# Eight more transpose sets in 64 by 64 tiles, and the steps reordered around them, in a retention and WaveMLP kernel

## The chip, the cores and the metric

The kernel runs on one core of a Trainium2 chip. The metric is the device time of one execution in microseconds (us). The engines are named as the profile names them: PE is TensorE (matmul, and transposes as matmuls against an identity), PEld its weight loads, DVE is VectorE, ACT is ScalarE, POOL is GpSimd, SP is SyncE, which here issues DMAs only. ACT and POOL issue some DMAs as well.

## The reference

A recurrent retention layer (4 batches, 8 heads, 768 positions, 64 numbers a head) feeds a mixing layer of width 512:

```
state = gamma[h] * state + outer(k[t], v[t])        # for each batch and head
y[t]  = (q[t] @ state) / sqrt(64)
x     = y, heads side by side                       # 4 x 768 x 512
theta = x @ w_theta
zr, zi = x * cos(theta), x * sin(theta)
u     = x + w_tok_r @ zr + w_tok_i @ zi             # mixes the 768 positions
out   = u + relu(u @ w_ch)
```

Inputs and output are float32.

## The kernel before

**Tiling.** The recurrence is computed in blocks. A *unit* n covers one batch, 256 positions and four heads: three blocks of positions (i = 0, 1, 2) and two halves of the heads (h) for each of four batches make 24 units. The mixing layer works on *chunks* C of 128 positions, 6 to a batch and 24 in all; output tiles t are numbered in the same way. The units 2m and 2m+1 make the chunks 2m and 2m+1.

**Steps of a unit.** `Lk`, `Lq`, `Lv` load k, q and v (tiles kqf and vf, 256 KB a load). `ck` casts k to bf16 (tile kqb), `cq` casts q, `cqs` casts q and multiplies it by its decay, `cv` does so for v (tile vb). `Tk` and `Tq` transpose k and q on PE with four 128 by 128 transposes each; `E` empties the result from PSUM into kqT. Some units go another way: `Dk` transposes by a DMA, and `Tk6`, `Tq6`, `E6` do what `Tk`, `Tq`, `E` do in 64 by 64 tiles, below. `A` multiplies k by q (sixteen 64 by 64 products, tile at_ps), `m` masks it (DVE, tile at). `ST` makes the block's state (r_ps), `S0` and `S1` add it to the running state (s2), `SB` casts that state into a block-diagonal tile (sbd), `I` multiplies it by q, and `Y` adds at times vb. `XA` (times a decay, qx) or `XB` (a plain copy, if q was scaled by `cqs`) takes the result from PSUM into xT.

**Steps of a chunk.** `Tx` and `Ex`, `Tx6` and `Ex6`, or a transposing DMA `Dx` bring xT into x_sb. `Hh` multiplies xT by w_theta (four products, th_ps); `CN` takes sine and cosine (ACT, tile cs, two calls of 128x512); `z` multiplies them by x. `Tw`, `Tw6` and `Ew`, `Ew6` transpose the token weights, one set for each 128 columns of the two matrices. `M.t.s` is one sixth of output tile t (two products, y_ps), `u` adds x, `Tu`, `Tu6` or a transposing DMA `Du` transposes u, `O` multiplies by w_ch, `f` adds the relu, `SO` stores. The last tile is done in halves (`Mh`, `uh`, `Tuh`, `Oh`, `fh`). `Z` is an empty product on zeros that feeds nothing.

**64 by 64 tiles.** `tiles64` (line 331) does each 128 by 128 transpose as four transposes of 64 by 64, each on a quarter of the array. The results go to two PSUM tiles, one for each half of the source's partitions, and each is emptied by its own copy. PSUM tiles of transposes come from a pool with two buffers (tag "tr"): a full set takes one of them, a set in 64 by 64 tiles takes both. `A`, `ST` and `Y` use 64 by 64 tiles anyway.

**Order.** Nothing is scheduled by rule. The table ORDER lists some 940 steps by hand; the last part of a name tells the engine (v DVE, a ACT, p POOL) or the queue of a load or store (s SP, a ACT). Each engine and each queue runs its own steps in the order of the table and waits in place. So a load on SP that stands behind a transposing DMA also waits for what that DMA waits for. PSUM banks for `Hh`, `M` and `O` come from a pool of two (tag "acc").

**Constants.** const3 computes the small decays (qsc, vsc) and const8 and const9 the large one (qx) with exponentials on ACT; const7 is one small sine, so that the sine's table is loaded there. An exponential and a sine need different tables; the load is an instruction of its own.

## Time and profile before

| | |
|---|---|
| median of 3 runs | 164.59 us (164.54 to 165.16) |
| span of the profiled execution | 163.3 us |
| granted clock of PE | 1.000 |
| bytes moved by DMA | 35.19 MB |

The time of the profiled execution itself is not given; the runs lie 1.2 to 1.9 us above its span, the median 1.3. The page lists busy time by engine and the costliest groups of instructions. Matmuls are pipelined: the duration of one holds some time in which the next runs already, so the cost of a step on PE is read from the start of one group to the start of the next. The other engines overlap neighbours by a little less than 0.1 us.

### The profile page before, as it was taken

To read this page: it belongs to the slowest core of one execution; us is meant where nothing else is said; L and a number is where in the kernel's file an instruction comes from. 1 tells how busy PE (TensorE), PEld (TensorE's weight loads), DVE (VectorE), ACT (ScalarE), POOL (GpSimd) and SP (SyncE) were. 2 spreads that over 40 slices of the span, in tenths; PEclk is the share of its full clock that TensorE was granted. 3 is DMA by queue.
4 is the path that set the end of the run, shared out by engine and by line. 5 is a ranking of instruction groups with operands and counts; after the bars stand their busy time and mean duration, and the time that the engine had idled before them with its cause. 6 is when DMAs were issued, how large, how long until landed. Compare 5 with 4: busy or idle time off the path is not lost.

```text
span 163.3 us, 5070 instructions
## 1 busy us (share of the span) xinstructions
PE 154.7 (95%) x2100; PEld 85.5 (52%) x2100; DVE 114.5 (70%) x217; ACT 78.8 (48%) x147; POOL 74.3 (45%) x106
## 2 busy tenths in 40 slices
PE   5996989999999998999999999999999999999992
PEld 1454646656666654644544655455545554444561
DVE  3388687987994786794999787698867760345362
ACT  4966698983658264673423645822341616000020
POOL 7657289176514770520057689910469204600000
PEclk9999999999999999999999999999999999999999
DMA  4999999999999999999999999999896527514446
GB/s 116 297 290 252 258 294 240 277 220 285 226 162 275 296 205 220 251 207 245 335 236 172 242 195 305 222 192 276 185 251 129 101 64 225 161 68 128 128 156 230
DMA packets 70118, 35.19 MB, mean 215 GB/s; under 512 B 27472, under 2 KB 67152, under 8 KB 70096
## 3 DMA queue, kind: packets, MB, share of 16 engines
q1 hardware_dynamic: 57088, 24.00, 68.6%
q10 hardware_dynamic: 10320, 7.47, 16.6%
q0 software_dynamic: 2688, 3.41, 12.1%
q8 instruction: 16, 0.26, 0.7%
q14 instruction: 6, 0.05, 0.1%
HBM read 25.69 MB, written 6.29 MB: 196 GB/s over the span
## 4 chain that ended last, share of the span: by engine, by line
PE 79%; DMA 7%; DVE 6%; POOL 4%; issue 1%; ACT 1%; DVEq 0%; POOLq 0%
PE y_ps L559 33%; PE o_ps L595 10%; PE th_ps L511 10%; PE zz L279 5%; PE r_ps L458 4%; PE at_ps L380 4%; DMA x_sb<-xT 4%; DMA kqT<-kqb 3%; PE kq_ps L318 3%; PE w_ps L533 2%; DVE at L389 2%; POOL z L525 2%; PE r_ps L446 2%; PE y_ps L620 2%; PE r_ps L408 1%
## 5 line engine op out<-in xcount | busy, mean ns | idle before, releaser
L559 PE MATMUL y_ps<-z,wtr 128*128 128x512 bf16 x138 | 52.4, 380 | 0.0
L559 PE MATMUL y_ps<-z,wti 128*128 128x512 bf16 x138 | 52.3, 379 | 0.0
L525 POOL TENSOR_TENSOR z<-cs,x_sb 128x1024 bf16<-128x1024 bf16 x12 | 25.5, 2135 | 17.7 <-ACT cs L518 10.8
L389 DVE TENSOR_TENSOR at<-at_ps,mask 128x1024 bf16<-128x1024 f32 x24 | 29.2, 1215 | 0.5 <-PE at_ps L380 0.5
L310 POOL TENSOR_TENSOR vb<-vf,vsc 128x512 bf16<-128x512 f32 x15 | 15.6, 1045 | 21.7 <-ACT sbd L136 11.7
L601 DVE SCALAR_TENSOR_TENSOR ot<-o_ps,u 128x512 f32<-128x512 f32 x22 | 15.1, 688 | 13.6 <-PE o_ps L595 13.5
L511 PE MATMUL th_ps<-wth,xT 128*128 128x512 bf16 x96 | 24.5, 380 | 0.0
L566 DVE TENSOR_TENSOR u<-y_ps,x_sb 128x512 bf16<-128x512 f32 x23 | 15.8, 688 | 10.9 <-PE y_ps L559 10.5
L595 PE MATMUL o_ps<-wch,uT 128*128 128x512 bf16 x88 | 22.6, 380 | 0.0
L518 ACT ACTIVATE cs<-th_ps,halfpi 128x512 bf16<-128x512 f32 x24 | 16.3, 682 | 11.8 <-PE th_ps L511 7.0
L518 ACT ACTIVATE cs<-th_ps,zerob 128x512 bf16<-128x512 f32 x24 | 16.4, 684 | 10.6 <-PE th_ps L511 5.1
L559 PEld LDWEIGHTS <-wtr 128*128 128x128 bf16 x138 | 13.5, 98 | 13.4
L559 PEld LDWEIGHTS <-wti 128*128 128x128 bf16 x138 | 13.5, 98 | 12.7 <-issue 0.4
L138 POOL CAST sbd<-s 64x256 bf16<-64x256 f32 (+1 forms) x20 | 8.4, 418 | 24.3 <-DVE s L426 22.1
L136 ACT COPY kqT<-kq_ps 128x1024 bf16<-128x1024 bf16 (+1 forms) x10 | 9.7, 969 | 9.8 <-PE kq_ps L318 9.5
L511 PEld LDWEIGHTS <-xT 128*128 128x128 bf16 x96 | 8.7, 98 | 8.5
L279 PE MATMUL zz<-zero 128*128 128x512 bf16 x30 | 10.8, 495 | 1.9 <-DVE zero L191 1.9
L595 PEld LDWEIGHTS <-uT 128*128 128x128 bf16 x88 | 8.1, 98 | 8.4 <-issue 0.2
L136 ACT CAST kqb<-kqf 128x512 bf16<-128x512 f32 x16 | 9.6, 620 | 5.5 <-DMA kqf<-in_k_dram 5.4
L458 PE MATMUL r_ps<-at,vb 64*64 64x128 bf16 x384 | 10.0, 221 | 1.6 <-DVE at L389 1.6
L380 PE MATMUL at_ps<-kqT 64*64 64x128 bf16 x384 | 10.0, 220 | 1.1 <-DVE kqT L138 0.6
L476 DVE TENSOR_TENSOR xT<-r_ps,qx 128x256 bf16<-128x256 f32 x22 | 8.7, 417 | 1.8 <-PE r_ps L458 0.8
(88 smaller groups left out, 209.4 us busy)
## 6 DMA issues: line engine op xcount, KB each, us to landing
vf<-in_v_dram SPq DMA_DIRECT2D x20, 256.0 KB, 5.7
kqf<-in_k_dram SPq DMA_DIRECT2D x19, 256.0 KB, 5.4
kqf<-in_q_dram SPq DMA_DIRECT2D x17, 256.0 KB, 5.7
out_dram<-ot ACTq DMA_DIRECT2D x12, 256.0 KB, 2.5
out_dram<-ot SPq DMA_DIRECT2D x11, 256.0 KB, 2.4
kqf<-in_q_dram ACTq DMA_DIRECT2D x7, 256.0 KB, 5.4
kqf<-in_k_dram ACTq DMA_DIRECT2D x5, 256.0 KB, 6.7
vf<-in_v_dram ACTq DMA_DIRECT2D x4, 256.0 KB, 5.7
```

Source lines behind the costliest of these rows:

```text
L136: nc.scalar.copy(dst, src)
L279: nc.tensor.matmul(t[:m, :cols], K["zero"][:, :m], K["zero"][:, :cols], start=True, stop=True)
L310: engines[e].tensor_mul(in_blocks(vb), by_token(raw["vf", n]), _bcast_last(K["vsc"][:, i, :, h * HU:(h + 1) * HU], D))
L380: nc.tensor.matmul(at_ps[cols, g, j, a, :], kq_at(n, 0, a, j, c)[rows], kq_at(n, 1, slice(0, 2), j, c)[rows], start=(j == 0 and a == 0), s ...
L389: nc.vector.tensor_mul(at.rearrange("p g j a t -> p (g j) (a t)"), st["at_ps", n].rearrange("p g j a t -> p (g j) (a t)"), _bcast_mid(K["m ...
L458: nc.tensor.matmul(st["R", n + 1][c][g * D:(g + 1) * D, j * P:(j + 1) * P], st["vb", n][rows, lo:lo + D], st["at", n][rows, g, j, a, :], s ...
L511: nc.tensor.matmul(th_ps, st["xT", C][:, j, :], K["wth"][:, j, :], start=(j == 0), stop=(j == 3))
L518: nc.scalar.activation(st["cs", C][:, w, :], st["th_ps", C], AF.Sin, bias=K["zerob" if w else "halfpi"], scale=1.0)
L525: engines[e].tensor_mul(st["z", b][:, c], st["cs", C], _bcast_mid(x_of(C), 2))
L559: nc.tensor.matmul(st["y", t], K["wT"][r][:, s0, t0 * P:(t0 + 1) * P], st["z", b][:, s0, r, :], start=(done == 0 and r == 0), stop=(done = ...
L566: nc.vector.tensor_add(st["u", t], st["y", t], st["x", b][:, t0, :])
L595: nc.tensor.matmul(o_ps, st["uT", t][:, j, :], K["wch"][:, j, :], start=(j == 0), stop=(j == nD - 1))
```

## The change

The functions that do the work are the same. What changes is the table: 936 steps become 944. Two new functions, `SP` and `I6`, stand in the code and are not in the table. Line numbers shift by one, and by 17 behind the new functions.

- **Sets in 64 by 64 tiles.** k and q of units 0 to 3 (`Tk`, `Tq`, `E` become `Tk6`, `Tq6`, two `E6` each), `Tw.1.2` and `Tw.1.4`. Chunks 1, 8 and 15 use `Tx6`, and chunk 12 goes back to `Tx`: two more. For u the four sets in 64 by 64 tiles are now 0, 3, 5 and 8, before 4, 5, 8 and 11.
- **Fewer changes of tiling.** In the order of the table PE changes between full tiles and 64 by 64 tiles 60 times from the first set to the last, before 68 times.
- **Engines.** z of chunks 0, 13, 15, 22 and 23 goes from POOL to DVE; many casts and copies change engine. Units 0, 7, 9, 12 and 21 take `cq` and `XA` where they had `cqs` and `XB`, and units 5, 6 and 19 the other way round.
- **Order.** Almost every step stands elsewhere. The loads on SP keep their order up to the loads of unit 12.

```diff
-const2 Lv.0.s const1 const6.v Z.29 Z.2 const5 Z.38 Lk.0.a const3 Z.35 Z.8 Lq.0.s Lv.1.s Z.28 constA
-const4 Lq.1.a const9 Lk.1.s Z.39 const8 ck.0.p Tk.0 ck.1.a cqs.0.v cv.0.v Tq.0 E.0.v Lq.4.a ST.0 Lk.4.a
...
+Lv.0.s Lk.0.a const2 const1 Lq.0.s Z.3 Z.11 const5 Lv.1.s ck.0.v Z.23 Lq.1.a cq.0.v const3 Lk.1.s Z.38
+Lq.4.a constA const4 const7 cqs.1.p cv.0.v Z.15 Tk6.0 const8 ST.0 Tq6.0 const6.v Z.18 E6.0.0.a Z.8
...
+    def SP(n, e):
+        _, i, h = unit(n)
+        c0 = 0 if i else 1
+        st["sp", n] = work.tile([P, 2, 2, D], BF, name="sp", bufs=3)
+        copy(e, st["sp", n][:, c0:], st["s2", n][:, c0:])
+
+    def I6(n):
+        r = R_of(n + 1)
+        for pair in (((0, 1), (1, 0)), ((0, 0), (1, 1))):
+            for j in range(2):
+                for g, c in pair:
+                    rows = slice(g * D, (g + 1) * D)
+                    nc.tensor.matmul(r[c][rows, j * P:(j + 1) * P], st["sp", n][rows, c, j, :],
+                                     kq_at(n, 1, slice(0, 2), j, c)[rows],
+                                     start=(j == 0), stop=False, skip_group_check=True)
```

Two places as the built programs have them. First the start of ACT's queue, before. (qsc and vsc are const3, qx is const8 and const9, one is const7; a row named DMA is a load that ACT issues.)

```order
L239 ACT_TABLE_LOAD
L239 ACTIVATE qsc<-arg,lscale 128x48
L239 ACTIVATE vsc<-arg,zerob 128x48
L156 DMA kqf<-in_q_dram 128x4x128
L232 ACTIVATE qx<-pos,lscale,lgp 128x512 x4
L232 ACTIVATE qx<-pos,lscale,lgp 128x256 x4
L136 CAST kqb<-kqf 128x512
L156 DMA kqf<-in_q_dram 128x4x128
L156 DMA kqf<-in_k_dram 128x4x128
L136 COPY kqT<-kq_ps 128x1024
```

And now, the same queue:

```order
L240 ACT_TABLE_LOAD
L240 ACTIVATE qsc<-arg,lscale 128x48
L240 ACTIVATE vsc<-arg,zerob 128x48
L157 DMA kqf<-in_q_dram 128x4x128
L252 ACT_TABLE_LOAD
L252 ACTIVATE one<-zerob,halfpi 128x1
L233 ACT_TABLE_LOAD
L233 ACTIVATE qx<-pos,lscale,lgp 128x256 x4
L137 COPY kqT<-kq_ps 128x512 x2
L157 DMA kqf<-in_k_dram 128x4x128
L233 ACTIVATE qx<-pos,lscale,lgp 128x512 x4
```

The sine has moved from behind the exponentials to between them, so that two more table loads stand in the queue (the fourth follows later, ahead of the first `CN`); the load of q of unit 4 has moved ahead of the exponentials, and that of k of unit 4 stays behind the first eviction.

Second, the queue of SP around the load of q of unit 10, which is the same before and now but for the numbers. Now (u_1280 is u.1, kqf_1399 is q of unit 10, kqf_1440 q of unit 14):

```order
L157 DMA kqf_1152<-in_k_dram 128x4x128
L607 DMA_TRANSPOSE uT_1342<-u_1280 128x4x128
L157 DMA kqf_1399<-in_q_dram 128x4x128
L607 DMA_TRANSPOSE uT_1429<-u_1292 128x4x128
L157 DMA kqf_1440<-in_q_dram 128x4x128
```

What moved is its user. On PE before, `Tq.10` (kqb_1158) stands behind two steps of M.4 (y_ps_1320):

```order
L559 MATMUL y_ps_1320<-z_738,wtr_101 128x512
L559 LDWEIGHTS wti_102
L559 MATMUL y_ps_1320<-z_738,wti_102 128x512
L318 LDWEIGHTS kqb_1158
L318 MATMUL kq_ps_1315<-ident_159,kqb_1158 128x128
```

And now (kqb_1328) behind `Tk.10` and the first step of M.3 (y_ps_1451):

```order
L319 LDWEIGHTS kqb_1328
L319 MATMUL kq_ps_1446<-ident_158,kqb_1328 128x128
L576 LDWEIGHTS wtr_103
L576 MATMUL y_ps_1451<-z_839,wtr_103 128x512
L576 LDWEIGHTS wti_104
L576 MATMUL y_ps_1451<-z_839,wti_104 128x512
L319 LDWEIGHTS kqb_1328
L319 MATMUL kq_ps_1446<-ident_158,kqb_1328 128x128
```

`Tq.10` has moved ahead of all other steps of M.3 and of the whole of M.4. At the same time the last step of M.1, for which u.1 waits, has moved back behind `A.8`; before, it stood ahead of `Tk.8`.

## The prediction

> **What bounds the kernel now.** I read the page's busy shares first, then the windows by stretch, then TensorE's (PE's) own timeline with its waits, and last the queues in front of the two places where PE waits.

> ```profile
> PE 154.7 (95%) x2100; PEld 85.5 (52%) x2100; DVE 114.5 (70%) x217; ACT 78.8 (48%) x147; POOL 74.3 (45%) x106
> ```
> ```profile
> 8.00:12.00 4.00, 3.79 (x90) 2.33 (x88) 3.24 (x7) 2.39 (x5) 2.15 (x4) 1.00 1.22 290
> 12.00:16.00 4.00, 2.50 (x66) 1.58 (x66) 3.14 (x7) 3.00 (x6) 3.18 (x5) 1.00 1.20 258
> 22.20:32.00 9.80, 9.56 (x172) 6.07 (x172) 8.43 (x17) 9.12 (x16) 6.26 (x8) 1.00 1.17 268
> 32.00:64.00 32.00, 32.00 (x429) 18.87 (x426) 25.66 (x51) 19.11 (x33) 16.98 (x16) 1.00 1.16 237
> ```
> The columns are the stretch, its length, then busy time and count of PE, PE's weight loads, DVE, ACT, POOL, then the granted clock, the DMA share and GB/s. From 32 on PE never rests and the clock is 1.00: there each microsecond of PE work is a microsecond of time. Ahead of 22 PE rests or is fed with empty products; between 22 and 32 ACT is busy 9.12 of 9.80 and sets the pace as much as PE does.

> ```profile
> L279 PE MATMUL zz<-zero 128*128 128x512 bf16 x30 | 10.8, 495 | 1.9 <-DVE zero L191 1.9
> ```
> ```profile
> 14.27 0.42 PE L458 MATMUL r_ps<-at,vb 64*64 64x128 bf16 x16 [1.11 <-DVE at L389]
> 21.68 0.42 PE L458 MATMUL r_ps<-at,vb 64*64 64x128 bf16 x16 [0.47 <-DVE at L389]
> 31.41 1.03 PE L511 MATMUL th_ps<-wth,xT 128*128 128x512 bf16 x4
> 64.90 0.42 PE L380 MATMUL at_ps<-kqT 64*64 64x128 bf16 x16 [0.49 <-DMA kqT<-kqb]
> ```
> The bracket is PE's idle time ahead of the row and what ended it. The third row is Hh.4, my milestone. The fourth is the longest wait after it.

> **The change part by part.** *Transposes and tiling.* What a set costs, and what a change of tiling costs:

> ```profile
> 38.53 0.61 PE L318 MATMUL kq_ps<-ident,kqb 128*128 128x128 bf16 x8
> 38.98 0.38 PE L559 MATMUL y_ps<-z,wtr 128*128 128x512 bf16 x1
> ...
> 68.12 0.42 PE L337 MATMUL kq_ps<-ident,kqb 64*64 64x64 bf16 x32
> 68.37 0.31 PE L408 MATMUL r_ps<-vb,kqb 64*64 64x64 bf16 x16
> ```
> ```profile
> 65.32 0.22 PE r_ps L458 x16
> 77.52 3.02 PE y_ps L559 x14
> 80.55 0.35 PE r_ps L458 x16
> 81.55 0.97 PE o_ps L595 x4
> 152.35 0.86 PE o_ps L595 x4
> ```
> From start to start, k and q of one unit cost 0.45 in full tiles and 0.25 in 64 by 64 tiles. In the second fence (the chain of waits: start, length) the same sixteen products take 0.22 behind 64 by 64 work and 0.35 behind full tiles, and the same four 0.97 against 0.86: 0.13 to enter, 0.11 to leave. Four k, q sets give 4 x 0.20 = 0.8; two x sets half as much each, 0.2; two weight sets of 24 small transposes (24 of 32 of the 0.25, 0.19) instead of 6 full ones (6 of 8 of the 0.45, 0.33) 0.14 each, 0.3: together 1.3. By the order table PE's tiling changes 60 times now, 68 before; 8 x 0.12 = 0.9. Sum: 2.2 of PE work less. But when I add PE's steps in program order by these durations, Hh.4 has 126.5 of work behind it before and 126.3 now. So 2.0 of the 2.2 lie ahead of Hh.4, where other things pace the kernel; they count only as far as those chains get shorter.

> *Evictions.* A set is now emptied in two halves, and both banks of the pool are taken.

> ```profile
> L136 ACT COPY kqT<-kq_ps 128x512 bf16<-128x512 bf16 x1 | 0.6, 585 | 0.3 <-PE kq_ps L337 0.3
> L136 ACT COPY kqT<-kq_ps 128x1024 bf16<-128x1024 bf16 x9 | 9.1, 1011 | 9.5 <-PE kq_ps L318 9.5
> L136 ACT CAST kqb<-kqf 128x512 bf16<-128x512 f32 x16 | 9.6, 620 | 5.5 <-DMA kqf<-in_k_dram 5.4
> L136 ACT CAST sbd<-s 64x256 bf16<-64x256 f32 x12 | 4.8, 403 | 1.9 <-DVE s L426 1.7
> L136 ACT CAST xT<-r_ps 128x256 bf16<-128x256 f32 x17 | 5.9, 374 | 7.1 <-DVE s L426 4.7 <-PE r_ps L408 1.2 <-PE r_ps L458 1.1
> ```
> Two halves cost ACT 1.17 instead of 1.01, 0.16 a set. Where the PE has other work (after Hh.4) this is covered by it; without that cover it is 0.16 a set.

> *ACT's tables.* const7 (the sine that loads its table early) now stands ahead of the exponentials of const8 and const9, so the order on ACT has four table loads, not two.

> ```profile
> 1.67 1.28 ACT L239 ACT_TABLE_LOAD   x1 [1.67 <-DVE arg L216]
> 13.48 1.28 ACT L251 ACT_TABLE_LOAD   x1
> 23.23 0.69 ACT L518 ACTIVATE cs<-th_ps,zerob 128x512 bf16<-128x512 f32 x1
> 23.81 0.68 ACT L518 ACTIVATE cs<-th_ps,halfpi 128x512 bf16<-128x512 f32 x1
> ```
> The second and third load (2.57) stand while the first inputs are still landing; the fourth stands straight ahead of the first sine, behind unit 3's xT. It is on the path, since ACT is the full engine there: 1.28. [...]

> *From the fifth unit's q to Hh.4.* In the vector queue cqs.5 now stands ahead of S0.4 and m.4, so all wait for q of unit 5.

> ```profile
> 3.21 0.32 ACT L239 ACTIVATE vsc<-arg,zerob 128x48 f32<-128x48 f32 x1
> 8.70 0.44 ACTq L156 DMA_DIRECT2D kqf<-in_q_dram  x1
> 9.18 0.53 ACTq L156 DMA_DIRECT2D kqf<-in_k_dram  x1
> 15.85 0.37 SPq L156 DMA_DIRECT2D kqf<-in_k_dram  x1
> 16.26 0.51 SPq L156 DMA_DIRECT2D kqf<-in_q_dram  x1
> ```
> ```profile
> DMA to landing us min/median/max: 5.7/5.7/5.7
> ```
> ```profile
> 6.07 0.69 DVE L304 TENSOR_TENSOR kqb<-kqf,qsc 128x512 bf16<-128x512 f32 x1 [3.11 <-DMA kqf<-in_q_dram]
> 22.26 0.29 DVE L426 TENSOR_TENSOR s<-r_ps,s 128x128 f32<-128x128 f32 x1 [0.63 <-PE r_ps L408]
> ```
> The first fence is ACT's and SP's, the second the landing of q of unit 5: 16.26 and 5.7, so 21.96. The third has DVE's price of a scaled cast and of a state add. SP issues k of unit 5 (15.85) and q behind it only when k of unit 4 (9.18) has landed. Now q of unit 4 is issued right behind vsc, at 3.5 instead of 8.70, so one load less stands in k of unit 4's way: 0.26 MB at 290 GB/s (first window) is 0.9. Bounds: 0, if only bytes count, and 1.6, if all SP loads move up as far as k of unit 4 can. I take 1.2, nearer to the upper end, since the windows show GB/s falling from 290 to 258 while SP waits: there is room. So q lands at 20.8, cqs.5 and S0.4 end at 21.7 (0.69 and 0.29). Then ACT in its new order, each about 0.1 less than its row because neighbours overlap (23.23 to 23.81 is 0.58 for a 0.69): sbd 0.32, two xT 0.56, table 1.28, sines of C 1 1.17, kqb 0.52, sines of C 0 1.17, sbd 0.32, kqT 0.92, sines of C 2 and C 3 2.44: 8.7. Hh.4 needs the bank that C 3's sines empty: 30.4 against 31.41. With 0.2 less work behind it: **1.2 gained**, 0.0 if q lands as before, 1.6 at best.

> *q of unit 10.* Here the reordering puts something on the path. On SP this load stands behind the transposing DMA Du.1, which waits for u.1, the vector add behind the last product of M.1.

> ```profile
> 42.71 0.68 DVE L566 TENSOR_TENSOR u<-y_ps,x_sb 128x512 bf16<-128x512 f32 x1
> 43.42 1.28 SPq L590 DMA_TRANSPOSE uT<-u  x1
> 44.80 0.53 SPq L156 DMA_DIRECT2D kqf<-in_q_dram  x1
> 52.32 1.04 POOL L304 TENSOR_TENSOR kqb<-kqf,qsc 128x512 bf16<-128x512 f32 x1
> 55.21 0.39 PE L318 MATMUL kq_ps<-ident,kqb 128*128 128x128 bf16 x4
> ```
> ```profile
> DMA to landing us min/median/max: 6.2/6.2/6.2
> ```
> ```profile
> DMA to landing us min/median/max: 4.2/4.2/4.2
> ```
> The rows are u.1, Du.1, the load, cqs.10 and Tq.10; the landing of this load, and that of the next one (issued 48.21). The chain is fixed: 0.2 for the product's end, u.1 0.7, Du.1's issue 1.4, landing, cqs.10 1.05, with 0.1 for hand-overs 3.5 plus the landing, 7.7 to 9.7. In the order table PE had 13.6 of work between the last product of M.1 and Tq.10: hidden, as 55.21 against the landing at 51.0 shows. Now M.1 ends later and Tq.10 comes earlier: M.2 four times (1.73; a step M is two products of 0.216, the 3.02 for fourteen above), Hh.6, Hh.7, O.0 (2.59), Tx.6, Tk.9, Tq.9, Tk.10 (0.89), Tw.0.3, I.8 (0.56), one 64 by 64 group (1.0), M.3.0 (0.43): 7.2. PE, in order, waits 0.5 to 2.5 with everything behind it. I take 5.2 for the landing, midway: **1.5 lost**. Nothing else ahead of PE has so short a lead.

> *What comes back.* A wait on PE lets the DMA chains behind it catch up:

> ```profile
> 59.39 5.47 DMA kqT<-kqb
> ```
> This transfer made the 0.49 at 64.90. cq.11 now runs on POOL and issues it some 0.5 later within its chain, but PE is later by more: I count the 0.5 back. z of five chunks moves from POOL to DVE, which at 25.66 of 32 (fourth window) has room; I put it at 0, with bounds of -0.5 (the size of the one wait that a late buffer made) and +0.5.

> Sum against the profiled execution: 163.3 - 1.2 + 1.5 - 0.5 = 163.1. The runs' median of 164.59 lies 1.3 above its span: **164.4**.

> **The rivals.** *The load is hidden after all.* If it lands in 4.2, as the next one did, the wait is 0.5; with 1.2 to 1.6 from the front and the 0.5 back: 163.0 to 163.4, say 163.2. For it: the row of 4.2. Against: the load beside it took 6.2 while a large weight load was still running.

> *The loads do not come earlier* (slower). q of unit 5 lands at 21.96 again, Hh.4 starts at 31.5 and gains 0.1; u.1 is then as late as PE, and with a landing of 6.2 Tq.10 waits 2.5; 0.5 comes back: 164.6 - 0.1 + 2.5 - 0.5 = 166.5, or 165.8 with a middling landing; I say 166.0. It decides from a q of unit 5 later than about 21.6. For it: DMA share over 1.1 in every window to 64. Against: the falling GB/s. [...]

> *The change does not save what it says*: the two-bank sets make PE wait for both halves of each eviction, 0.16 by the rows above for each of the eight sets, 1.3 on top of the 164.4: 165.7. Against: after Hh.4 PE has other work ahead of each next set.

> **How the numbers follow.** Within 0.5% (163.8 to 165.4, about what a measurement of this kernel can tell from no change) lies the forecast, 0.36; the hidden load, faster, 0.36; the loads that stay, 0.20, and the double eviction, 0.08, slower, 0.28. The range of eight in ten runs from 163.0 to 166.0; the forecast's own is 163.8 to 165.2.

> **What would show it.** Right: PE's longest wait after 32 is ahead of Tq.10 at about 52, ended by POOL's kqb; no wait at A.11; four table loads, the last just ahead of the first cs; Hh.4 near 30.4. Wrong: Tq.10 without a bracket, Hh.4 after 31, or long waits of PE ended by kqT, x_sb or z between 60 and 150.

## The result, and the profile after

The changed kernel takes 169.35 us (median of 4 runs, 168.99 to 169.92), the kernel before 164.56 (4 runs): a ratio of 1.0289, 95% interval 1.0256 to 1.0322. It is slower by 4.8 us, where 164.4 was forecast. Times and ratios below leave out runs that lie over 1.5% above the fastest of their kernel (two of four in a_full, one of four in b_many, two of six in b_t6_01 and in b_tail, one of six in b_t6_01z and in b_t6_23z); a ratio can still differ a little from the quotient of two medians.

The page after gives the busy time and the clock of PE in 40 slices of 4.2 us:

```profile
PE 153.1 (92%) x2225; PEld 86.2 (52%) x2256; DVE 121.2 (72%) x231; ACT 74.2 (44%) x141; POOL 66.4 (40%) x108
...
PEclk9999579999999999999999999999999999999998
```

The span is 4.0 longer (167.3 against 163.3). What grew is rest, and work at a lower clock. How much less PE works cannot be read from this page: 31 of its 2256 products are missing in this trace (x2225, against x2256 weight loads), while the trace before has all of its 2100. The windows, with the columns of those before:

```profile
12.00:16.00 4.00, 2.21 (x92) 1.42 (x83) 3.58 (x9) 3.56 (x8) 1.91 (x2) 1.00 1.21 293
16.00:22.20 6.20, 4.94 (x118) 3.52 (x122) 3.21 (x8) 2.36 (x7) 2.87 (x4) 0.52 1.19 267
22.20:32.00 9.80, 9.04 (x171) 6.18 (x167) 8.87 (x16) 8.40 (x17) 5.89 (x10) 0.96 1.05 253
32.00:64.00 32.00, 31.08 (x520) 19.07 (x524) 27.60 (x56) 17.46 (x32) 16.85 (x21) 1.00 1.16 218
```

From 16 to 22.2 PE ran at a granted clock of 0.52, and from 32 to 64 it rests 0.92 (a little of it where products are missing) where it did not rest at all. PE's timeline has the places:

```profile
16.39 0.26 PE L409 MATMUL r_ps<-vb,kqb 64*64 64x64 bf16 x3 [0.53 <-DVE xT L139]
17.19 0.38 PE L409 MATMUL r_ps<-vb,kqb 64*64 64x64 bf16 x12 [0.54 <-issue]
...
23.39 0.38 PE L280 MATMUL zz<-zero 128*128 128x512 bf16 x1
...
29.20 1.02 PE L528 MATMUL th_ps<-wth,xT 128*128 128x512 bf16 x3 [0.56 <-ACT cs L535]
...
33.53 1.03 PE L528 MATMUL th_ps<-wth,xT 128*128 128x512 bf16 x3
...
39.74 0.38 PE L576 MATMUL y_ps<-z,wtr 128*128 128x512 bf16 x1 [0.21 <-ACT cs L535]
...
53.41 0.38 PE L319 MATMUL kq_ps<-ident,kqb 128*128 128x128 bf16 x4 [0.23 <-DVE wti L139]
...
54.07 0.39 PE L319 MATMUL kq_ps<-ident,kqb 128*128 128x128 bf16 x4
...
73.15 1.02 PE L528 MATMUL th_ps<-wth,xT 128*128 128x512 bf16 x3 [0.23 <-DVE ot L618]
...
82.87 0.42 PE L381 MATMUL at_ps<-kqT 64*64 64x128 bf16 x16 [0.22 <-DMA kqT<-kqb]
...
86.97 0.32 PE L409 MATMUL r_ps<-vb,kqb 64*64 64x64 bf16 x16 [0.30 <-DVE xT L493]
...
109.56 0.32 PE L409 MATMUL r_ps<-vb,kqb 64*64 64x64 bf16 x16 [0.59 <-POOL vb L311]
```

Hh.4 (fifth row) starts at 33.53, before at 31.41: 2.1 of the 4.0 are lost ahead of it. The six bracketed rows behind it add up to 1.78, and no other wait there is over 0.2: they are the rest. So there are two questions, the front and six small waits; the front is the larger and was forecast with the wrong sign.

The second row is the clue. It is in the middle of ST.2, behind the fourth of its sixteen products, with nothing to wait for: "issue" means that no event that the profile shows ended the pause.

### The profile page after: what moved, and what is told of

It is laid out like the page before. It is cut to its first block, busy times and chain, and to the rows that moved or that the text cites. A ratio compares the mean times of both kernels' runs of the same rounds, so it can differ in the third digit from the quotient of the medians.

```text
span 167.3 us, 5372 instructions
## 1 busy us (share of the span) xinstructions
PE 153.1 (92%) x2225; PEld 86.2 (52%) x2256; DVE 121.2 (72%) x231; ACT 74.2 (44%) x141; POOL 66.4 (40%) x108
## 3 DMA queue, kind: packets, MB, share of 16 engines
q10 hardware_dynamic: 10320, 7.47, 16.2%
## 4 chain that ended last, share of the span: by engine, by line
PE 56%; DMA 15%; DVE 14%; ACT 6%; issue 3%; POOL 2%; SPq 1%; ACTq 0%; DVEq 0%; POOLq 0%
PE y_ps L576 27%; DMA kqf<-in_k_dram 9%; PE o_ps L612 8%; PE th_ps L528 6%; DVE at L390 4%; DMA kqT<-kqb 4%; DMA kqf<-in_q_dram 3%; PE r_ps L475 3%; ACT cs L535 2%; PE at_ps L381 2%; DVE z L542 2%; PE r_ps L447 2%; PE r_ps L409 2%; PE y_ps L637 2%; DVE xT L493 2%
## 5 line engine op out<-in xcount | busy, mean ns | idle before, releaser
L576 PE MATMUL y_ps<-z,wtr 128*128 128x512 bf16 x136 | 51.6, 380 | 0.6 <-ACT cs L535 0.2
L576 PE MATMUL y_ps<-z,wti 128*128 128x512 bf16 x128 | 48.5, 379 | 0.3 <-issue 0.3
L535 ACT ACTIVATE cs<-th_ps,zerob 128x512 bf16<-128x512 f32 x24 | 16.4, 685 | 14.8 <-PE th_ps L528 13.9
L612 PE MATMUL o_ps<-wch,uT 128*128 128x512 bf16 x83 | 22.2, 380 | 0.5 <-issue 0.2
L535 ACT ACTIVATE cs<-th_ps,halfpi 128x512 bf16<-128x512 f32 x24 | 16.5, 686 | 13.5 <-PE th_ps L528 11.4
L311 POOL TENSOR_TENSOR vb<-vf,vsc 128x512 bf16<-128x512 f32 x17 | 18.0, 1062 | 10.4 <-DMA vf<-in_v_dram 10.1
L542 POOL TENSOR_TENSOR z<-cs,x_sb 128x1024 bf16<-128x1024 bf16 x7 | 14.9, 2125 | 7.5 <-ACT cs L535 5.3
L542 DVE TENSOR_TENSOR z<-cs,x_sb 128x1024 bf16<-128x1024 bf16 x17 | 13.7, 813 | 2.6 <-ACT cs L535 2.2
L139 POOL CAST kqb<-kqf 128x512 bf16<-128x512 f32 x18 | 11.6, 653 | 3.4 <-DMA kqf<-in_k_dram 2.4
L137 ACT CAST sbd<-s 64x256 bf16<-64x256 f32 (+1 forms) x22 | 8.0, 364 | 11.0 <-DVE s L427 10.8
L381 PE MATMUL at_ps<-kqT 64*64 64x128 bf16 x384 | 11.0, 227 | 1.9 <-ACT kqT L137 1.4
L280 PE MATMUL zz<-zero 128*128 128x512 bf16 x25 | 9.7, 507 | 2.3 <-DVE zero L192 1.9
L137 ACT CAST xT<-r_ps 128x256 bf16<-128x256 f32 x17 | 6.0, 370 | 11.5 <-PE r_ps L409 7.0
```

Source lines behind the costliest of these rows:

```text
L137: nc.scalar.copy(dst, src)
L139: engines[e].tensor_copy(dst, src)
L311: engines[e].tensor_mul(in_blocks(vb), by_token(raw["vf", n]), _bcast_last(K["vsc"][:, i, :, h * HU:(h + 1) * HU], D))
L381: nc.tensor.matmul(at_ps[cols, g, j, a, :], kq_at(n, 0, a, j, c)[rows], kq_at(n, 1, slice(0, 2), j, c)[rows], start=(j == 0 and a == 0), s ...
L535: nc.scalar.activation(st["cs", C][:, w, :], st["th_ps", C], AF.Sin, bias=K["zerob" if w else "halfpi"], scale=1.0)
L542: engines[e].tensor_mul(st["z", b][:, c], st["cs", C], _bcast_mid(x_of(C), 2))
```

## The experiments

PE's program is a list of rows; a weight load is one and a product is one. I count them from the start, and leave the waits out that are instructions of their own in PE's program (17 before, 20 after): a k, q set is 16 rows in full tiles and 64 in 64 by 64 tiles. PE's program has 4200 rows before and 4512 after; 192 of the 312 more are the sets of units 0 to 3.

### The first four: clock, one wait, and the sets

**Holding the clock (a_hold).** Three more empty products where PE waited.

```diff
-A.1
+Z.40 A.1
...
-Y.1 XB.1.1.v Lq.5.s ST.2
+Z.41 Y.1 XB.1.1.v Lq.5.s Z.42 ST.2
```

> The kernel after, with three more empty products (Z) where PE waited: ahead of A.1 (0.64), of Y.1 (0.77) and of ST.2 (0.53). They feed nothing. Clock theory: the kernel after loses its 2 us ahead of Hh.4 because PE's granted clock is 0.50 from 16.4 to 23.4, and the clock falls because PE rests too much from 12 to 17; then the clock stays at 1.00, Hh.4 starts near 31.7 instead of 33.5, and the time falls by about 2, to 167.4. Chain theory: the evictions, casts and DVE's queue set the pace there and the slow clock only slows a PE that waits; then Hh.4 stays at or after 33.2 and the time stays within 0.5 of 169.35, whatever the clock does.

170.28, ratio 1.0405 (1.0334 to 1.0476). The clock held, and neither the time fell nor did Hh.4 come earlier (33.89; in the kernel after 33.53):

```profile
16.00:22.20 6.20, 4.16 (x129) 2.48 (x128) 4.42 (x9) 2.66 (x7) 4.16 (x6) 1.00 1.18 261
```
```profile
16.66 0.39 PE L280 MATMUL zz<-zero 128*128 128x512 bf16 x1 [0.48 <-issue]
...
22.86 0.23 PE L507 MATMUL x_ps<-ident,xT 128*128 128x128 bf16 x1 [2.15 <-issue]
...
56.53 0.40 PE L319 MATMUL kq_ps<-ident,kqb 128*128 128x128 bf16 x4 [1.98 <-POOL kqb L305]
```

At full clock PE now stands still for 2.15 at 20.7, again for "issue", in the middle of Tx.0. The clock theory falls as the cause of the front's loss: what a slow clock took (0.52 from 16 to 22.2), a pause took when the clock was full (1.00 there). The third row is Tq.10, the wait of the prediction; its 1.98 is in the time of a_hold and not in that of the kernel after, so Hh.4 is the fairer measure of the front. It comes back below.

**ST.2 ahead of XB.1.1 (a_st2).**

```diff
-Y.1 XB.1.1.v Lq.5.s ST.2
+Y.1 ST.2 XB.1.1.v Lq.5.s
```

> The kernel after, with ST.2 ahead of the copy XB.1.1 again (as the kernel before has it), so that ST.2 does not wait for that copy (0.53, and 0.54 behind its first products). Chain theory: m.2 starts 0.8 to 1.0 earlier and the time falls by about as much, to 168.4. Clock theory: PE is fed a little better, but the clock falls all the same; 0.3 or less is gained.

169.58, ratio 1.0327 (1.0292 to 1.0362): no gain. The wait for xT is gone, and the pause in the same place is longer:

```profile
16.91 0.29 PE L409 MATMUL r_ps<-vb,kqb 64*64 64x64 bf16 x12 [1.02 <-issue]
...
23.70 0.60 PE L280 MATMUL zz<-zero 128*128 128x512 bf16 x2 [1.59 <-issue]
```

The pauses stand at fixed rows. In the kernel after and in a_st2 the first is behind the fourth product of ST.2, whose first row is 437: row 445. The second in a_st2 is at Z.27, row 701. In a_hold 8 and 12 rows more stand ahead, and the pauses move to Z.42 (row 445) and to Tx.0's fourth product (row 703). 445 and 701 are 256 rows apart. The view of DMA queues has one queue called "instruction"; in the kernel after, two stretches of 0.2 us show one packet each, 14.4 to 14.6 and 20.8 to 21.0:

```profile
q8 instruction: 1, 0.02, 37.4%
```
```profile
q8 instruction: 1, 0.02, 29.0%
```

The rows drift by a few against the pauses, because the waits are not counted. Counted with them, from 0 and from PE's first instruction, the pauses end at instruction 450, 706, 962 or 2754, all 16 of them: exact multiples of 256 apart. (In the kernel after, where products are missing, the first one recorded behind the pause is 451.)

**The other side: before with fewer fillers (b_starve).**

```diff
-Z.34 cv.2.p
+cv.2.p
...
-Z.18 XB.0.0.v
+XB.0.0.v
...
-Z.23 XB.1.0.v
+XB.1.0.v
```

> The kernel before, without three of its empty products (Z.34, Z.18, Z.23, which run between 10.9 and 15.5). Nothing reads them. Clock theory: PE rests more between 11 and 16, its clock falls to 0.50 for several us as in the kernel after, Hh.4 starts 1.5 to 2 later than 31.4 and the time rises to about 166.5. Chain theory: the time stays within 0.5 of 164.56, clock or no clock, since PE waits for others there.

165.14 against 164.40, ratio 1.0061 (1.0031 to 1.0090). The clock fell, and cost 0.7, not 2:

```profile
14.00:16.00 2.00, 1.18 (x51) 0.82 (x39) 1.55 (x4) 0.69 (x3) 1.23 (x2) 0.76 1.23 243
16.00:18.00 2.00, 2.00 (x17) 1.42 (x14) 1.84 (x4) 0.37 (x1) 1.17 (x2) 0.50 1.14 170
```

**Full tiles for units 0 to 3 (a_full).**

```diff
-Tk6.0
+Tk.0
...
-E6.0.0.a
...
-E6.0.1.a
+E.0.a
...
```

> The kernel after, with k and q of units 0 to 3 in full 128 by 128 tiles again and one eviction each (units 0 to 2 on ACT, 3 on DVE) at the place of the later half. Theory that the 64 by 64 sets do the harm (two evictions one behind the other make A.0 and A.1 about 0.6 late): Hh.4 starts 0.6 or more earlier and the time falls to 168.7 or less. Theory that they save what they were costed at: 0.8 more PE work, of which some is covered, time 169.4 to 170.1. Clock theory: 0.8 more PE work between 6 and 18 may hold the clock; if the granted clock is 1.00 from 16 to 23 here, the time falls by 2, else it hardly moves.

166.67 (two runs, 166.64 and 166.69) against 164.40, ratio 1.0155 (1.0113 to 1.0197). In its profile (span 164.8) no pause is marked issue and the clock is 0.998; row 445 is in ST.3. A.7 starts 2.1 earlier than in the kernel after (38.8 against 40.9, with the same work behind it): what the front had lost. With 0.8 more PE work (by the forecast's 0.2 a set) its span is 2.5 shorter. Hh.4 is back where it was before (31.41):

```profile
31.27 1.03 PE L527 MATMUL th_ps<-wth,xT 128*128 128x512 bf16 x4
```

What stays is 1.5 of span against before, now mostly a wait ahead of Hh.10 for a PSUM bank, which f.3 empties only when the store SO.0 has freed its buffer:

```profile
71.94 1.02 PE L527 MATMUL th_ps<-wth,xT 128*128 128x512 bf16 x4 [1.30 <-DVE ot L617]
```
```profile
71.20 0.69 DVE L617 SCALAR_TENSOR_TENSOR ot<-o_ps,u 128x512 f32<-128x512 f32 x1 [1.44 <-DMA out_dram<-ot]
```

### The code theory, tested on the kernel before

**More rows, the same work (b_many).** `Z.n.16` does a Z in 16 pieces of 64 columns: 32 rows instead of 4.

```diff
-Z.15 I.0 Z.27
+Z.15.16 I.0 Z.27.16
...
```

> The kernel before, with seven of its empty products between 9.6 and 18 (Z.15, 27, 34, 18, 23, 11, 3) cut into 16 pieces of 64 columns each instead of 2 of 512: the same columns through PE, 196 more instructions (32 instead of 4 each). Sets, order and evictions stay. Code theory: PE's program comes in blocks of 256 instructions by DMA; the stalls that the trace puts down to issue stand at PE rows 445 and 701 in the kernels after, a_hold and a_st2, each about 6 us behind the block before; here row 445 falls into Z.23, reached at about 15.5, and row 701 into Tx.1, about 20 (before: A.3 at 19.2, ST.5 at 27.2); so stalls marked issue appear at these two rows, the second of 1.5 to 3 us, and the time rises by 1.5 to 3. Clock theory and chain theory: nothing of that; at most 0.5 for fillers that run a little longer in pieces.

167.94 against 164.43, ratio 1.0206 (1.0126 to 1.0286). Sets, order and evictions are those of before; the pause is where the count puts it, in Z.23 behind five pieces (row 447), and there is one in the middle of the program that nobody had asked for, within six rows of row 2749 (at instruction 2754):

```profile
16.41 0.53 PE L279 MATMUL zz<-zero 128*64 128x64 bf16 x11 [0.60 <-issue]
...
88.47 0.38 PE L511 MATMUL th_ps<-wth,xT 128*128 128x512 bf16 x1 [1.49 <-issue]
```

The second one expected, at row 701, did not come: the block was there when PE was (its packet is at 18.3, Tx.1 at about 21).

**The sets alone (b_t6).**

```diff
-Tk.0
+Tk6.0
...
-E.0.v
+E6.0.0.v E6.0.1.v
...
```

> The kernel before, with k and q of units 0 to 3 in 64 by 64 tiles, evicted in two halves on the engine that did it in one (and Tx.0 behind unit 3's evictions, since it needs a bank); nothing else is changed: the change's first part alone. Code theory: 192 more PE instructions before Tx.0, row 445 falls into Tk.2 (about 15) and row 701 into Tx.1 (about 20): stalls marked issue there, time up by 1.5 to 3. The forecast's costs: 0.8 less PE work, partly covered, and 0.16 a set for the second eviction: within 0.6 of 164.5.

167.90, ratio 1.0215 (1.0153 to 1.0277): up by 3.5, with less PE work. Row 445 is in Tk.2, and again five products are through before the pause:

```profile
16.99 0.28 PE L337 MATMUL kq_ps<-ident,kqb 64*64 64x64 bf16 x11 [1.89 <-issue]
...
91.57 0.39 PE L559 MATMUL y_ps<-z,wtr 128*128 128x512 bf16 x1 [0.70 <-issue]
```
```profile
18.00:19.00 1.00, 0.91 (x17) 0.52 (x16) 0.80 (x4) 0.36 (x1) 0.35 (x1) 0.58 1.17 308
19.00:20.00 1.00, 1.00 (x26) 0.34 (x28) 1.00 (x2) 0.04 (x1) 0.00 (x0) 0.50 1.01 299
```

The pause comes first (it ends at 16.99), and work at a lower clock follows it, 0.58 from 18 and 0.50 from 19. The second pause, 0.70, was not expected; it is at instruction 2754, as in b_many.

**Two table loads (a_tab).**

```diff
-constA const4 const7 cqs.1.p
+constA const4 cqs.1.p
...
-S0.2.v ck.3.a A.2
+S0.2.v ck.3.a const7 A.2
```

> The kernel after, with the sine that loads its table (const7) behind the exponentials again (after the cast ck.3): two table loads instead of four. The forecast put 1.28 on the fourth load, on the path to Hh.4: then the time falls by 0.6 (the wait of Hh.3 for ACT's sine, 0.56) to 1.3. Code theory: PE stands at row 701 until about 23.4 whatever ACT does, but the sine comes behind it, so Hh.3's wait of 0.56 goes: 0.4 to 0.7.

168.55, ratio 1.0242 (1.0190 to 1.0294): 0.8 less than after, inside what was expected, but the two intervals overlap. Hh.4 shows it more clearly: 32.34 instead of 33.53. The first sine starts at 25.78 instead of 27.88 and Hh.3's wait for it is gone; the block of row 701 still ends a pause, at 22.64, and the next block one of 0.30, at 28.66:

```profile
22.64 0.59 PE L280 MATMUL zz<-zero 128*128 128x512 bf16 x2 [1.18 <-issue]
```

**Four waits taken out of a_full (a_best).**

```diff
-u.5 CN.9.1 ST.11 Lq.13.a SO.0.a
+u.5 SO.0.a CN.9.1 ST.11 Lq.13.a
...
-XA.13.0 ST.14
+ST.14 XA.13.0
...
```

(and the edits of a_st2 and a_tab.)

> The kernel a_full (k and q of units 0 to 3 in full tiles; its undisturbed profile had a span of 164.8) with four more edits: const7 behind the exponentials; ST.2 ahead of XB.1.1 and ST.14 ahead of XA.13.0 (waits of 0.53 and 0.51 in a_full); the store SO.0 ahead of the sines of chunk 9 in ACT's queue, since f.3 waited 1.44 for an output buffer that this store frees, and Hh.10 behind it 1.30. Code theory and these waits: no stall marked issue; 0.5 + 0.5 + 0.5 + 1.3 of waits gone, less what reappears behind: 163.5 to 165.5. If the reordering costs elsewhere, or the code still stalls: 166 or more.

167.27, ratio 1.0157 (1.0075 to 1.0239), as a_full. The four waits are gone, and no pause is marked issue; others stand in their place, the largest 0.99 at I.2 for ACT's sbd, which the moved table load delays, 0.72 for ACT's wti and 0.64 for u. The rest of the change without the sets of units 0 to 3 still costs 1.5%, and it hangs on no single one of these waits.

### Half the sets, and the end of the program

**Units 2 and 3 (b_t6_23), units 0 and 1 (b_t6_01).** The edit of b_t6 for two units each.

> The kernel before, with k and q of units 2 and 3 alone in 64 by 64 tiles (Tx.0 behind unit 3's evictions as in b_t6). Half of the sets of b_t6, and 96 more PE rows instead of 192. Code theory: a block of 256 rows is fetched from the time at which PE enters the block before it, and is ready some 6 us later; here row 189 is entered at 11.5 as before, so the block from row 445 (now in Tk6.3, about 17.3) is ready at 17.5, and the next (A.4, about 23.2) at 22.0 to 23.6: stalls of 0 to 0.7 in all, time 164.4 to 165.3, far less than half of b_t6's 3.4. Eviction theory (each set costs by its two evictions, and Tx.0 by its place): half of b_t6's loss or more, 166.0 to 166.5, with waits ended by kqT and none marked issue.

> The kernel before, with k and q of units 0 and 1 alone in 64 by 64 tiles: 96 more rows, all of them ahead of row 189. Code theory: row 189 is entered at about 10 instead of 11.5, so its successor from row 445 (A.2, about 16.2) is ready at about 16.5 to 17.2: a stall marked issue of 0.3 to 1.0 at A.2, and the time rises by as much, to 164.8 to 165.6. Eviction theory: half of b_t6's loss, 166.0 to 166.5, with waits ended by kqT at A.0 and A.1.

168.44, ratio 1.0251 (1.0203 to 1.0300), and 167.40, ratio 1.0200 (1.0143 to 1.0257): each as much as all four, which no theory had. In the first the pause stands where it should, 0.87 in Tk.3 at row 447. In the second none is marked: A.2 waits 0.39 for its eviction, as before, and at instruction 450, in the middle of A.2, 0.3 pass between two weight loads. What both share is the end: from DVE's last instruction to the end of the span it is 4.6, in before 2.9. Both programs have 4296 rows. PE enters a new block about row 4285 (4275 when the waits are counted too), with the last product of Oa.1, 1.7 ahead of its end; if that starts the fetch of one more block, it falls among the last stores, as the packet of b_tail below does.

**A longer end (b_t6_01z, b_t6_23z), and the length alone (b_tail).**

```diff
-Z.31
+Z.31.16
```

> The kernel b_t6_01 (units 0 and 1 in 64 by 64 tiles), with the last empty product cut into 16 pieces, so that PE's program has 4325 rows instead of 4297. Theory: b_t6_01 and b_t6_23 cost 3.6 and 3.8 not by their sets but by their length: 4297 rows end 12 rows behind a block boundary (row 4285), the next block is fetched at the very end, and the time from DVE's last instruction to the end of the span is 4.6 instead of 2.9. Then here it is 2.9 again and the time falls by about 1.7, to 165.5 to 166.5. Eviction theory (the sets cost it): no change, 168.2.

> The kernel b_t6_23 (units 2 and 3 in 64 by 64 tiles), with the same lengthening to 4325 rows. Theory of the end of the program: the time falls by about 1.7, to 165.0 to 166.8, with 2.9 behind DVE's last instruction. Eviction theory: no change, 168.4.

169.13, ratio 1.0280 (1.0224 to 1.0337), and 167.37, ratio 1.0171 (1.0128 to 1.0214). The edit missed: the rows were put behind Oh.1, so the block is still entered at the same place, and the end still takes 4.4 in both. Length as such is not it; the moment is. a_full and a_best (4320 rows) enter the block in a step of Mh, 3.5 ahead of PE's end; their packet is at 158.1 in a_full, ahead of the last stores, and the end takes 2.9. b_t6_23z has a second pause, 0.53 at instruction 706 (24.56), which b_t6_23 has not, and why b_t6_01z is slower than b_t6_01, whose steps it shares up to the last Z, is open.

```diff
-Z.29 Z.2 const5 Z.38
+Z.29.8 Z.2.8 const5 Z.38.8
...
-Z.31
+Z.31.8
```

> The kernel before, with the seven empty products that stand ahead of A.0 and the last one cut into 8 pieces instead of 2: 96 rows more, 4297 in all, the same sets, order and columns. Code theory: row 445 then falls into Z.11 (about 16.4) and is ready at about 15.9: no stall there; only the end changes, 4.6 behind DVE's last instruction instead of 2.9, and the time rises by 1.7 to about 166.2. If the length of the program does not matter: 164.4 to 165.0.

167.66 against 164.75, ratio 1.0204 (1.0141 to 1.0267). Nothing but the cut of eight empty products differs from before. A pause of 0.55 stands at Z.11, where row 445 is (not expected: the block was later than 15.9), and the end is 4.45 long, since the block is entered in Oh.1, 1.0 ahead of PE's end. First b_tail from 159 on, then before from 158 on:

```profile
q8 instruction: 1, 0.02, 1.3%
...
out_dram<-oh SPq DMA_DIRECT2D x1, 128.0 KB, 3.8
```
```profile
out_dram<-oh SPq DMA_DIRECT2D x1, 128.0 KB, 2.0
```

The last store lands in 3.8 instead of 2.0. 0.55 and 1.6 make 2.1 of the 2.3 by which its span is longer. From 163.0 to 164.2, shortly ahead of that landing, the DMA engines move 15 to 31 GB/s, against some 250 to 400 in use before, about what one of 16 would move by these figures; that it is the engine that had fetched the block is not shown.

**Beating both (b_a11).**

```diff
-A.11 Y.10 ck.14.v ST.11
+Y.10 ck.14.v ST.11 A.11
...
-Tk.19 Tq.19 CN.17.1 O.8
+O.8 Tk.19 Tq.19 CN.17.1
```

> An attempt to beat both: the kernel before, with A.11 behind Y.10 and ST.11 (0.35 of PE work ahead of the one wait of 0.49 for the transposing DMA of unit 11) and O.8 ahead of Tk.19 (the wait of 0.16 for its cast). Nothing else. If these waits are on the path: 0.4 to 0.5 less, 163.9 to 164.1. If the work behind them was waiting for something else: no change, 164.2 to 164.6.

164.11 against 164.65, ratio 0.9984 (0.9952 to 1.0015). Both waits are gone from the profile, and one of 0.36 for POOL's sbd stands at I.18; the interval holds 1, so it is not shown to be faster than before. No kernel here is.

## Why the prediction was wrong

**The step that failed** is the one from unit 5's q to Hh.4: "Hh.4 needs the bank that C 3's sines empty: 30.4 against 31.41." It measured 33.53, 3.1 later. Its premise held: the load was issued at 13.80 instead of 16.26, and cqs.5 did not wait for it.

```profile
24.09 0.68 DVE L305 TENSOR_TENSOR kqb<-kqf,qsc 128x512 bf16<-128x512 f32 x1
```

But that chain did not set the pace. PE itself arrived at I.3 at 23.82, before at 20.83, mostly because its own code was late. In the kernel after only 0.54 of this shows as a pause, and most of the rest is work at half clock (0.52 from 16 to 22.2); a_hold shows that at full clock (1.00) the pauses for code took as much, 0.48 and 2.15. The step took PE's rows as free: sets in 64 by 64 tiles were costed by their time (0.25 against 0.45, which is true) and not by their rows (64 against 16). The pauses at 445 and 701 show this directly; b_many (1.0206) and b_tail (1.0204) show that rows alone cost 2%, b_tail most of it at the end. a_full, with a quarter of the rows in these sets, has PE at I.3 at 21.02 and Hh.4 at 31.27: 2.3 of the 3.1 come back. The other 0.9 do not, so the gain of 1.2 that the step promised is not there even then. In a_best, which has two table loads and ST.2 early as well, Hh.4 starts at 30.63.

**Transposes and tiling.** The 2.2 of PE work less were not measured, since products are missing in the trace after. The work behind Hh.4 was given as 0.2 less, and there the kernel lost 1.9, nearly all by waits (133.8 from Hh.4 to the end against 131.9). The forecast had 0.8 more there.

**Evictions.** Taken at 0.16 a set and as covered after Hh.4, they show there in one wait, 0.23 at Tk.10 for a bank that two halves of wti hold. Ahead of Hh.4 A.0 and A.1 waited for kqT, 0.74 and 0.64, which the sum left out. But the second half is not what they waited for: in a_full, with one eviction a set, they waited 0.68 and 0.77. A.1 in the kernel after, then in a_full:

```profile
13.17 0.42 PE L381 MATMUL at_ps<-kqT 64*64 64x128 bf16 x16 [0.64 <-ACT kqT L137]
```
```profile
13.53 0.42 PE L380 MATMUL at_ps<-kqT 64*64 64x128 bf16 x16 [0.77 <-ACT kqT L136]
```

**Tables.** Right: four loads, the last straight ahead of the first sine.

```profile
26.59 1.28 ACT L535 ACT_TABLE_LOAD   x1
27.88 0.69 ACT L535 ACTIVATE cs<-th_ps,halfpi 128x512 bf16<-128x512 f32 x1
```

With two of them taken out in a_tab Hh.4 came 1.2 earlier, where the forecast had 1.28; in the time some 0.8 of it is left.

**Unit 10's q.** The mechanism was right and the size off. The load was issued at 48.90 and landed in 3.6, under the forecast's bounds of 4.2 to 6.2, so Tq.10 (54.07, above) has no bracket:

```profile
52.53 1.04 POOL L305 TENSOR_TENSOR kqb<-kqf,qsc 128x512 bf16<-128x512 f32 x1 [3.66 <-DMA kqf<-in_q_dram]
```

In a_hold, with the same order there, it landed in 5.2 (issued 50.26, cast from 55.43) and Tq.10 waited 1.98. The 1.5 was the price of a load of 5.2; a landing of 3.6 cost nothing here.

**The 0.5 at A.11** came back: A.11 has no wait. **z on DVE** shows in no wait over 0.2 but the 0.59 for POOL's vb and 0.30 for DVE's xT, which were not traced to it.

**The rivals.** That loads do not come earlier: they did. That unit 10's load is hidden: it was, and it did not make the kernel faster. The double eviction: 0.23 in one place after Hh.4; the waits ahead of A.0 and A.1 are there with one eviction too. No rival had the code, and none ended at 169.

**What stays open.** Of the 4.8 us, a_full gives back about half, by two runs. The other half belongs to the rest of the change: six waits of 0.2 to 0.6 in the kernel after, others when these are taken out. No single cause was shown for it.

## What to carry to other kernels

Count instructions too, not only their time: where PE had to wait for a block of 256 rows, it came 5.2 to 7.9 us behind the entry into the block before it, and smaller tiles that are faster (0.25 against 0.45 us) need four times the rows (64 against 16). Around these pauses the DMA share was high (1.21 from 14.5 to 17.19 in the kernel after, 1.18 from 16 to 22.2 in a_hold); that this is why a block takes so long was not tested. The pauses marked "issue" that stood 256 instructions apart were this here. Fillers, a full clock and one step moved did not mend them (0.48 and 2.15 in a_hold, 1.02 and 1.59 in a_st2); fewer rows in that stage did (none in a_full). A changed row count also shifts the block boundaries behind it: a pause in the middle of the program came with it in b_many (1.49) and b_t6 (0.70), and a longer end in b_tail (4.45 instead of 2.9).

## What was not expected of the hardware

- PE's code seems to be fetched one block ahead only. In the front the packet stood 1.8 to 5.2 us behind the entry into the block before it (19.2 to 21.0 in before, 17.19 to 20.8 after, 16.91 to 21.1 in a_st2, 9.2 to 14.4 in b_tail), and where PE waited there it went on 2.5 to 2.7 behind the packet. Late in the program the packet can stand ahead of the entry (133.0 and 135.9 in b_t6_23z), so what exactly starts a fetch is open.
- Where a boundary was entered 1.0 to 1.9 us ahead of PE's end, the end was 1.5 to 1.7 longer (4.4 to 4.6 behind DVE's last instruction in five kernels; 2.9 in the others, of which a_full and a_best enter it 3.5 ahead).
- The clock fell to 0.50 in the kernel after, where no single rest from 12 to 17 was longer than 0.77 (PE was busy for 2.21 of the 4 us from 12 to 16); before, with 2.50 of these 4 and one rest of 1.11, it stayed at 1.00. What sets it off was not shown. The work at 0.50 cost little: 0.7 us in b_starve, and by a_hold nothing in the kernel after, where the code was late anyway.
